# Larger token chunks, weight low parts on VectorE and 64x32 array tiles for the scores, in attention followed by two gated layers

## The chip, the cores and the metric

One core of a Trainium2 chip. The metric is the device time of one execution in microseconds (us), the median of several runs. A core has TensorE (PE, products; its weight loads are listed as PEld), VectorE (DVE), ScalarE (ACT), GpSimd (POOL) and SyncE (SP, which here only issues the DMAs). Each engine takes its instructions in the order in which the program lists them; semaphores make one engine wait for another.

## The reference

```python
# B, H, SL, SG, D = 4, 8, 512, 32, 64
s_g = scale * q_g @ k_all.T                    # 32 global queries see all 544 keys
out_g = softmax(s_g) @ v_all
s_ll = where(|i - j| <= 32, scale * q_l @ k_l.T, -1e9)   # local queries see a band
s_l = concat([scale * q_l @ k_g.T, s_ll])      # and the 32 global keys
out_l = softmax(s_l) @ concat([v_g, v_l])
x = attention output as (2304 tokens, 512)     # here 17 tiles of 128 tokens are processed
h = x @ w_in;  x = (h * clip(h + 3, 0, 6) / 6) @ w_out     # layer 1, d_ff 2048
h = x @ w_in2; x = where(h > 0, h, exp(min(h, 0)) - 1) @ w_out2   # layer 2
```

The inputs are float32, but the weights arrive as float64. The batch of 4 has 16 tiles of 128 local queries and one tile with all 128 global queries: 17 tiles, 2176 tokens.

## The kernel before

**Products.** A float32 operand is split into a high part (float32r) and a low part, the rest; a product is three matmuls: high by high, high by low, low by high (`mm3`, L385 to L389). All products of the two layers stand on L389 and differ by tile: `h` is the first product of a layer (`up`), `acc` the second (`down`).

**Chunks.** The 17 tiles are processed in chunks, `CHUNKS = [3, 3, 3, 2, 3, 3]`. For each chunk a layer makes one pass over d_ff in 16 steps (f) of 128. A step has `up` (12 matmuls with the chunk's tokens as columns: 384 or 256), an activation, and `down` (in layer 1 four blocks of 3 matmuls with the tokens as columns; in layer 2 one block of 3 matmuls with 512 columns per tile), which runs `LAG = 2` steps after its `up`. Between the parts of a step are three gaps: after `up`, after the first half of `down`, and after its second half. All work that isn't a product is written into these gaps by hand (the loop at L532): stages of attention for the next chunk's tiles (`during`, L487), ticks of splitting weights, loads.

**Activation of a step.** ACT makes g from h (L403 in layer 1; L406, L407 in layer 2), DVE finishes it (L404, L408), ACT writes the high part gh (L409), and the low part gl = g - gh (L411) is made by POOL in chunk 0 of layer 1 and by DVE elsewhere. `down` waits for gl.

**Weights.** One slot holds 128 of d_ff: 512 columns' worth of w_in and of w_out, 1 MB as float64 words. `Split` makes float32 from these words and then a high and a low part: `first` (ACT, L100), `second` (DVE, L104), `third` (DVE, L108 and L111), `fourth` (ACT copies the high part, L121; POOL subtracts the low part in two halves, L123). `tick` (L129) runs two such stages of neighbouring slots. Slots 0 and 1 of layer 1 are split by halves before the first product, the others during chunk 0, one slot per step and two steps ahead of their use. Layer 2's slots are split from step 4 of layer 1's last chunk on, at one and a half ticks a step.

**Attention of a local tile** (class `Local`, L159) has six stages. `scores` twice (L198; half of the heads each): 8 matmuls of a 128-row operand, q laid out block-diagonally for the two heads of a pair, into 64 output rows (column tiles of 64), 128 keys as columns; each float32 matmul is two records in the trace. Then a masked reduction (DVE, L218), the exponential with its sum (ACT, L222), 1/sum (DVE, L225, L226) and the scaling of P (POOL, L229; DVE for the tiles before the first product). `transposed` twice (four transposes L74, an ACT copy L239). `values` (L242): 32 matmuls in column tiles of 32, 64 value columns each, an ACT copy of x (L256). `turned`: four transposes, the ACT cast x1h (L263), the DVE subtraction x1l (L264). The tiles of chunk 0 do this before the first product, in the order of the string `PRO` (L38); the other tiles in the gaps of the chunk before theirs, at places (0, 2, 4, 7, 9, 11) with a step of 6 from tile to tile (L481), so that neighbouring tiles interleave. A global job (class `Global`) has three stages; `GLOBALS` says how many run in which chunk.

**Buffers and queues.** PSUM has 8 banks: 4 `acc`, 2 `h`, 2 `att`. The stages during the chunks use `att`. Tiles before the first product lie in the buffers of the weight slots (`w`). When a chunk ends, its accumulators are copied to `ev` (four buffers; ACT L437 and DVE L439 by turns) and stored; layer 1's results go to DRAM and come back as layer 2's input. SyncE issues all DMAs in program order.

Of the kernel before, what the change touches and what calls it, by code (L numbers as in the profile page):

```python
# [10 lines left out]
F32 = mybir.dt.float32  # L11
# [31 lines left out]
# A float64's upper word, read as float32, has the upper 8 of its 11 exponent bits as its exponent;  # L43
# times this it has them less 896 = 1023 - 127.
# [9 lines left out]
def tile_kernel(ctx, tc, qkW, vW, qkG, vN, vG, masks, w1, w2, out):  # L54
# [10 lines left out]
    msk = pool.tile([P, 3, 2, P], F32, name="msk")  # L65
# [63 lines left out]
    def tick(m, times=1):  # L129
        """The next two stages of splitting the weights of layer m, of slots that follow each other."""  # L130
# [28 lines left out]
    class Local:  # L159
        """Attention of 128 local queries, all heads, cut into stages."""  # L160

        def __init__(self, n):
# [3 lines left out]
            self.p = {}  # L166

        def load_qk(self):
            tag, bufs = ("w", NF) if self.early else ("qk", 1)
            qk = pool.tile([P, 2, 2, 2 * P + WIN], F32, name=f"qk{self.n}", tag=tag, bufs=bufs)  # L170
            src = qkW[self.b, self.t]
            if self.n == 0:
                nc.sync.dma_start(qk[:, 0], src[:, 0])
                nc.sync.dma_start(msk, masks)
                nc.sync.dma_start(qk[:, 1], src[:, 1])
            else:
                nc.sync.dma_start(qk, src)
# [12 lines left out]

        def buffer(self, name, tag, part):
            if not self.early:
                return pool.tile([P, 2, 2, P], F32, name=name, tag=tag, bufs=2)
            if not self.p:
                self.room = pool.tile([P, 4, 2, 2, P], F32, name=f"room{self.n}", tag="w", bufs=NF)
            return self.room[:, 2 * (tag == "pt") + part]

        def scores(self, part, tag):  # L198
            """Two pairs of heads: rows are (block of a half, head of the pair, query)."""
            sp = bank([P, 2, 2, P], f"S{self.n}_{part}", tag)  # L200
            for j in range(2):
                for i in range(4):
                    r = i % 2 * 64
                    nc.tensor.matmul(  # L204
                        sp[r : r + 64, j, i // 2, :],
                        self.q[:, part, j, i, :],
                        self.k[:, part, j, 32 * i : 32 * i + P],
                        start=True,
                        stop=True,
                    )  # L210
            p = self.buffer(f"P{self.n}_{part}", "p", part)
            mn = pool.tile([P, 4], F32, name=f"mn{self.n}_{part}", tag="mn", bufs=2)
            sums = pool.tile([P, 4], F32, name=f"sums{self.n}_{part}", tag="sums", bufs=2)
            mi = 0 if self.t == 0 else (2 if self.t == TPB - 1 else 1)
            for j in range(2):
                for hf in range(2):
                    c = slice(2 * j + hf, 2 * j + hf + 1)
# [10 lines left out]
            pf = p.rearrange("p j f k -> p (j f) k")  # L228
            eng.tensor_tensor(pf, pf, sums.unsqueeze(2).to_broadcast([P, 4, P]), op=ALU.mult)  # L229
            self.p[part] = p  # L230

        def transposed(self, part, tag):
            p = self.p[part]
            tp = bank([P, 2, 2, P], f"T{self.n}_{part}", tag)
            for j in range(2):
                for hf in range(2):
                    transpose(tp[:, j, hf, :], p[:, j, hf, :])
            pt = self.buffer(f"PT{self.n}_{part}", "pt", part)
            nc.scalar.copy(pt, tp)  # L239
            self.p[part] = pt  # L240
# [420 lines left out]
```

## Time and profile before

| | |
|---|---|
| median of 3 runs | 925.02 us (923.87 to 925.42) |
| span of the profiled execution | 923.7 us |
| difference, for what lies around the span | 1.3 us |
| start of the first product of layer 1 | 32.55 us |
| windows of layer 1, chunks 0 to 5 | 104.22, 88.28, 86.92, 65.09, 82.98, 67.58 us |
| first chunk of layer 2 | 527.62 to 601.25, 73.63 us |
| busy: PE, DVE, ACT, POOL | 883.6, 411.6, 424.1, 183.6 us |

The profile gives no time of the profiled execution other than its span, so the span stands for it. A window of a chunk runs from its first `up` matmul to that of the next chunk; it holds 16 ups of the chunk, 14 of its downs and the last 2 downs of the chunk before. Matmuls overlap in the array, so the price of one is the distance between starts and not its duration.

### The profile page before, as it was taken

The numbers are of one execution on the slowest core, as the hardware profiler recorded it, in microseconds if no ns is written. First come the engines' busy times: TensorE is split into PE (matmuls) and PEld (weight loads), VectorE is DVE, ScalarE is ACT, GpSimd is POOL, SyncE is SP. The second block draws the span as 40 slices with busy tenths as digits, with TensorE's granted clock in tenths as the row PEclk, the third lists the DMA queues.
The fourth block names the chain that finished last, engine by engine and source line by source line (L and its number), as shares of the span: only waits on it lengthen the run. The fifth ranks groups of instructions, "written<-read, shape, count | busy, mean of one in ns | idle before, by whom it ended". The sixth has DMA issues, their size and how long they took to land.

```text
span 923.7 us, 15740 instructions
## 1 busy us (share of the span) xinstructions
PE 883.6 (96%) x6432; PEld 811.8 (88%) x6432; DVE 411.6 (45%) x911; ACT 424.1 (46%) x944; POOL 183.6 (20%) x124
## 2 busy tenths in 40 slices
PE   6588799999999999999999989999999999999998
PEld 4477799989989999999999979999999999989997
DVE  4988864332432343432339978432222232322222
ACT  5666645433532354443335566533443444434433
POOL 0489781100100010000006644300100101001000
PEclk9799899999999999999999989999999999999999
DMA  9766313331423235232056630020010020100100
GB/s 371 319 270 225 135 47 109 131 122 45 134 80 130 65 124 164 89 101 67 1 179 238 259 140 18 18 69 0 1 57 1 1 69 1 57 1 1 35 1 34
DMA packets 21816, 90.27 MB, mean 98 GB/s; under 512 B 2544, under 2 KB 5872, under 8 KB 17264
## 3 DMA queue, kind: packets, MB, share of 16 engines
q1 hardware_dynamic: 21744, 89.27, 27.1%
q8 instruction: 50, 0.82, 0.4%
q14 instruction: 22, 0.18, 0.1%
HBM read 80.35 MB, written 8.91 MB: 97 GB/s over the span
## 4 chain that ended last, share of the span: by engine, by line
PE 80%; DVE 10%; ACT 5%; issue 4%; POOL 1%; DMA 0%; ACTq 0%; DVEq 0%
PE acc L389 36%; PE h L389 36%; DVE f L108 4%; DVE f L111 3%; PE S L204 3%; DVE f L104 1%; PE O L248 1%; PE T L74 1%; DVE g L404 1%; ACT P L222 1%; PE SG L316 1%; ACT room L222 1%; PE OG L346 1%; ACT w L121 1%; ACT gh L409 0%
## 5 line engine op out<-in xcount | busy, mean ns | idle before, releaser
L389 PE MATMUL acc<-gh,w 128*128 128x384 f32 (+1 forms) x768 | 213.9, 337 | 0.0
L389 PE MATMUL h<-x1h,w 128*128 128x384 f32 (+1 forms) x768 | 209.6, 338 | 4.0 <-POOL w L123 2.8
L389 PE MATMUL h<-x2h,w 128*128 128x384 f32 (+1 forms) x768 | 203.5, 330 | 0.0
L389 PE MATMUL acc<-w,gh 128*128 128x512 f32 x544 | 171.9, 397 | 3.3 <-ACT ev L437 3.3
L409 ACT CAST gh<-g 128x384 fp32r<-128x384 f32 (+1 forms) x192 | 95.1, 495 | 153.9 <-DVE g L404 90.9
L389 PEld LDWEIGHTS h<-x1h,w 128*128 128x128 f32 x768 | 140.0, 191 | 10.1 <-POOL w L123 3.5
L389 PEld LDWEIGHTS acc<-gh,w 128*128 128x128 f32 x768 | 139.3, 189 | 5.0 <-issue 3.8
L389 PEld LDWEIGHTS h<-x2h,w 128*128 128x128 f32 x768 | 138.7, 189 | 4.1
L408 DVE SCALAR_TENSOR_TENSOR g<-g,h 128x384 f32<-128x384 f32 (+1 forms) x96 | 51.1, 532 | 199.2 <-ACT g L407 199.2
L389 PE MATMUL h<-x1l,w 128*128 128x384 f32 (+1 forms) x384 | 127.6, 332 | 4.5 <-DVE x1l L264 4.5
L411 DVE TENSOR_TENSOR gl<-g,gh 128x384 fp32r<-128x384 f32 (+1 forms) x176 | 95.6, 543 | 77.1 <-ACT gh L409 77.0
L389 PE MATMUL acc<-gl,w 128*128 128x384 f32 (+1 forms) x384 | 126.9, 330 | 2.6 <-POOL gl L411 2.6
L123 POOL TENSOR_TENSOR w<-f,w 128x512 fp32r<-128x512 f32 x64 | 110.9, 1753 | 89.7 <-ACT w L121 89.7
L389 PE MATMUL h<-x2l,w 128*128 128x384 f32 (+1 forms) x384 | 126.7, 330 | 0.0
L404 DVE SCALAR_TENSOR_TENSOR g<-g,h 128x384 f32<-128x384 f32 (+1 forms) x96 | 50.9, 530 | 154.7 <-ACT g L403 154.6
L389 PEld LDWEIGHTS acc<-w,gh 128*128 128x128 f32 x544 | 101.1, 190 | 19.4 <-ACT ev L437 3.6
L406 ACT ACTIVATE g<-h 128x384 f32<-128x384 f32 (+1 forms) x96 | 45.5, 474 | 145.2 <-PE h L389 145.2
L403 ACT ACTIVATE g<-h,half 128x384 f32<-128x384 f32 (+1 forms) x96 | 53.9, 562 | 119.2 <-PE h L389 116.5
L389 PE MATMUL acc<-w,gl 128*128 128x512 f32 x272 | 108.1, 398 | 0.0
L464 POOL TENSOR_TENSOR x2l<-x2raw,x2h 128x768 fp32r<-128x768 f32 (+1 forms) x12 | 21.9, 1823 | 325.2 <-ACT x2h L463 325.2
L229 POOL TENSOR_TENSOR P<-P,sums 128x512 f32<-128x512 f32 x26 | 31.2, 1198 | 246.0 <-DVE sums L226 221.3
L389 PEld LDWEIGHTS h<-x1l,w 128*128 128x128 f32 x384 | 73.3, 191 | 4.9 <-DVE x1l L264 4.9
(72 smaller groups left out, 918.8 us busy)
## 6 DMA issues: line engine op xcount, KB each, us to landing
raw<-in_w SPq DMA_DIRECT2D x32, 1024.0 KB, 6.7
qk<-in_qkW SPq DMA_DIRECT2D x15, 960.0 KB, 4.8
v<-in_vW SPq DMA_DIRECT2D x26, 512.0 KB, 4.9
qkG<-in_qkG SPq DMA_DIRECT2D x8, 608.0 KB, 3.8
vN<-in_vN SPq DMA_DIRECT2D x8, 512.0 KB, 4.7
out<-ev SPq DMA_DIRECT2D x16, 256.0 KB, 2.1
x2d<-ev SPq DMA_DIRECT2D x20, 192.0 KB, 2.1
x2raw<-x2d SPq DMA_DIRECT2D x10, 384.0 KB, 3.7
```

Of the source, the lines that this page charges most:

```text
L108: nc.vector.scalar_tensor_tensor(w, self.high[:, s], -0x80000000, w, op0=ALU.bitwise_and, op1=ALU.bitwise_or)
L111: nc.vector.scalar_tensor_tensor(w, self.low[:, s], 29, w, op0=ALU.logical_shift_right, op1=ALU.bitwise_or)
L123: nc.gpsimd.tensor_sub(lo[:, i], self.wf[:, i], hi[:, i].bitcast(F32))
L204: nc.tensor.matmul(sp[r : r + 64, j, i // 2, :], self.q[:, part, j, i, :], self.k[:, part, j, 32 * i : 32 * i + P], start=True, stop=True,)
L229: eng.tensor_tensor(pf, pf, sums.unsqueeze(2).to_broadcast([P, 4, P]), op=ALU.mult)
L389: nc.tensor.matmul(o, a, b, start=first and i == 0, stop=last and i == len(pairs) - 1)
L403: nc.scalar.activation(g, hp, AF.Relu, scale=1.0 / 6.0, bias=half)
L404: nc.vector.scalar_tensor_tensor(g, g, 1.0, hp, op0=ALU.min, op1=ALU.mult)
L406: nc.scalar.activation(g, hp, AF.Relu, scale=-1.0)
L408: nc.vector.scalar_tensor_tensor(g, g, -1.0, hp, op0=ALU.add, op1=ALU.max)
L409: nc.scalar.copy(gh, g)
L411: late.append(lambda: eng.tensor_sub(gl, g, gh.bitcast(F32)))
```

## The change

The chunks become 4, 3, 3, 3, 4 tiles, and layer 2 takes them in the order 1, 0, 2, 4, 3. Four tiles instead of three are attended to before the first product, in a new order. In layer 1 DVE instead of POOL subtracts the weights' low parts. A local tile has four stages: all scores in one, from a q without zeros, in eight array tiles of 64 rows by 32 columns whose row halves write to two banks; all eight transposes in one; values with a 65th column of ones, whose result is the sum of the exponentials, so that the scaling comes after the values; and the turning. Stages during the chunks stand at places (0, 4, 6, 8) with a step of 9, those of global jobs at (0, 3, 5) instead of (0, 4, 8).

```diff
-CHUNKS = [3, 3, 3, 2, 3, 3]
+CHUNKS = [4, 3, 3, 3, 4]
+ORDER2 = [1, 0, 2, 4, 3]
-PRO = "q0 q1 v0 q2 v1 00 01 10 02 11 03 20 v2 12 04 13 21 05 W4 14 a100 a200 a101 W a201 a300 15 22 a110 a111 a301 a400 a210 a211 a310 23 w1 24 a311 a401 w1 q3 25 a410 a411 w1 w1 w1 | W | | | | | w1 w1 | w1 | w1 v3 |"
+PRO = "q0 q1 v0 q2 v1 00 v2 10 01 q3 W4 20 11 02 a100 a200 v3 a101 a201 30 03 21 a300 12 a110 a111 a301 31 a400 22 13 a210 a211 a310 23 32 a311 a401 33 a410 a411 w1 w1 q4 w1 w1 | W | | | | | w1 w1 | w1 | w1 v4 |"
-GLOBALS = [0, 2, 3, 1, 2]
+GLOBALS = [0, 3, 3, 2]
...
-                nc.gpsimd.tensor_sub(lo[:, i], self.wf[:, i], hi[:, i].bitcast(F32))
+                (nc.gpsimd if self.m else nc.vector).tensor_sub(lo[:, i], self.wf[:, i], hi[:, i].bitcast(F32))
...
-        xh = pool.tile([P, KD, n], F32R, name=f"x{which}h{c}", tag="xh", bufs=2)
+        side = "ab"[c % 2 if which == 1 else 1 - ORDER2.index(c) % 2]
+        xh = pool.tile([P, KD, n], F32R, name=f"x{which}h{c}", tag=f"xh{side}", bufs=1)
...
-            qk = pool.tile([P, 2, 2, 2 * P + WIN], F32, name=f"qk{self.n}", tag=tag, bufs=bufs)
+            qk = pool.tile([P, NP, P + WIN], F32, name=f"qk{self.n}", tag=tag, bufs=bufs)
...
-            self.v = [pool.tile([P, TPB, 4, D], F32, name=f"v{self.n}_{i}", tag="v", bufs=2) for i in range(2)]
+            tag, bufs = ("w", NF) if self.early else ("vw", 1)
+            self.v = pool.tile([P, TPB, H, D + 1], F32, name=f"v{self.n}", tag=tag, bufs=bufs)
...
+            sp = [bank([P, NP, P], f"S{self.n}_{r}", tag) for r in range(2)]
+            for j in range(NP):
                 for i in range(4):
+                    for r in range(2):
+                        rs, cs = slice(64 * r, 64 * r + 64), slice(32 * i, 32 * i + 32)
+                        nc.tensor.matmul(
+                            sp[r][cs, j, :], self.q[rs, j, cs], self.k[rs, j, 32 * i : 32 * i + P],
+                            start=True, stop=True,
+                        )
+            for j in range(NP):
+                for r in range(2):
                     nc.vector.tensor_tensor_reduce(
+                        out=self.p[:, r, j, :], in0=sp[r][:, j, :], in1=msk[:, mi, :], scale=-SCALE, scalar=BIG,
+                        op0=ALU.add, op1=ALU.min, accum_out=mn[:, r, j : j + 1],
                     )
                     nc.scalar.activation(
-                        p[:, j, hf, :], p[:, j, hf, :], AF.Exp, scale=-1.0, bias=mn[:, c], accum_out=sums[:, c]
+                        self.p[:, r, j, :], self.p[:, r, j, :], AF.Exp, scale=-1.0, bias=mn[:, r, j : j + 1]
                     )
-            nc.vector.tensor_scalar_add(sums, sums, 1e-9)
-            nc.vector.reciprocal(sums, sums)
-            eng = nc.vector if self.early else nc.gpsimd
-            eng.tensor_tensor(pf, pf, sums.unsqueeze(2).to_broadcast([P, 4, P]), op=ALU.mult)
+        def transposed(self, tag):
+            for r in range(2):
+                tp = bank([P, NP, P], f"T{self.n}_{r}", tag)
+                for j in range(NP):
+                    transpose(tp[:, j, :], self.p[:, r, j, :])
+                nc.scalar.copy(self.pt[:, r], tp)
+        def values(self, tag):
+            op = [bank([P, NP, D + 1], f"O{self.n}_{r}", tag) for r in range(2)]
+            for r in range(2):
+                for j in range(NP):
+                    for i in range(4):
+                        cs = slice(32 * i, 32 * i + 32)
+                        nc.tensor.matmul(
+                            op[r][cs, j, :], self.pt[:, r, j, cs], self.v[:, i, 2 * j + r, :], start=True, stop=True
+                        )
+                nc.vector.tensor_scalar_add(sums[:, r], op[r][:, :, D], 1e-9)
+            nc.vector.reciprocal(sums, sums)
-            nc.scalar.copy(self.x, op)
+            for r in range(2):
+                nc.vector.tensor_tensor(
+                    self.x[:, :, r, :], op[r][:, :, :D], sums[:, r].unsqueeze(2).to_broadcast([P, NP, D]), op=ALU.mult
+                )
...
-        ev = pool.tile([P, n if m == 0 else DM], F32, name=f"ev{m}_{c}_{i}", tag="ev", bufs=4)
+        ev = pool.tile([P, n if m == 0 else DM], F32, name=f"ev{m}_{c}_{i}", tag="ev", bufs=3)
...
-            place, step = ((0, 2, 4, 7, 9, 11), 6) if isinstance(job, Local) else ((0, 4, 8), 6)
+            place, step = ((0, 4, 6, 8), 9) if isinstance(job, Local) else ((0, 3, 5), 6)
...
-        first = [locs[n].stages(tags=("acc", "acc", "att", "att", "h", "h")) for n in range(CHUNKS[0])]
+        first = [locs[n].stages(tags=("acc", "att", "h", "acc")) for n in range(CHUNKS[0])]
...
-        order = [list(range(NC)), [*range(NC - 2), NC - 1, NC - 2]]
+        order = [list(range(NC)), ORDER2]
```

The tiles p and pt of a stage go from two buffers to one each; the host's layout of q, k, v and the masks follows the new shapes.

## Rows read from the trace of the kernel before

**Rows 1.** The page's busy times; the chain of waits, 30 to 140 us, by line.

```profile
PE 883.6 (96%) x6432; PEld 811.8 (88%) x6432; DVE 411.6 (45%) x911; ACT 424.1 (46%) x944; POOL 183.6 (20%) x124
...
by line: DVE f L108 20.0%; DVE f L111 14.8%; issue 13.1%; DVE f L104 9.3%; ACT P L222 8.0%; PE acc L389 5.9%; PE h L389 5.8%; DVE g L404 5.1%; POOL w L123 4.1%; ACT gh L409 2.4%; POOL gl L411 2.2%; ACT w L121 2.2%; DVE sums L225 2.0%; DVE x
```

**Rows 2.** Windows: length, busy of PE, PEld, DVE, ACT, POOL (count), clock, DMA, GB/s.

```profile
32.55:136.77 104.22, 86.34 (x684) 78.65 (x685) 86.43 (x125) 59.78 (x121) 84.18 (x53) 0.92 0.49 183
136.77:225.05 88.28, 88.28 (x815) 81.56 (x815) 30.49 (x115) 37.36 (x102) 7.53 (x7) 1.00 0.32 106
225.05:311.97 86.92, 86.16 (x761) 79.38 (x761) 29.80 (x104) 33.71 (x86) 4.30 (x4) 1.00 0.29 98
...
377.06:460.04 82.98, 82.98 (x717) 77.36 (x715) 30.20 (x103) 34.00 (x91) 4.30 (x4) 1.00 0.20 65
460.04:527.62 67.58, 67.58 (x386) 67.58 (x386) 48.98 (x56) 33.89 (x50) 27.40 (x15) 1.00 0.61 217
527.62:601.25 73.63, 70.31 (x343) 63.92 (x343) 52.94 (x61) 43.12 (x71) 33.29 (x22) 0.95 0.20 68
```

**Rows 3.** Timeline of PE in layer 2 (start us, length us, instruction).

```profile
733.77 0.62 PE L389 MATMUL acc<-w,gh 128*128 128x512 f32 x2
...
735.87 0.28 PE L389 MATMUL h<-x2h,w 128*128 128x256 f32 x1
...
737.30 0.63 PE L389 MATMUL acc<-w,gh 128*128 128x512 f32 x2
```

**Rows 4.** Timeline of PE in chunk 1 of layer 1: stages of attention between products.

```profile
142.04 0.34 PE L389 MATMUL acc<-gh,w 128*128 128x384 f32 x1
142.31 1.09 PE L204 MATMUL S<-qk 128*64 128x128 f32 x16
...
143.61 0.34 PE L389 MATMUL h<-x1l,w 128*128 128x384 f32 x1
...
147.66 0.60 PE L74 MATMUL T<-ident,P 128*128 128x128 f32 x4
...
148.27 0.33 PE L389 MATMUL h<-x1l,w 128*128 128x384 f32 x1
...
161.61 1.10 PE L248 MATMUL O<-v,PT 128*32 128x64 f32 x64
...
162.92 0.34 PE L389 MATMUL acc<-gl,w 128*128 128x384 f32 x1
```

**Rows 5.** Timeline of DVE, ACT and POOL around the first products.

```profile
28.21 0.68 DVE L264 TENSOR_TENSOR x1l<-XT,x1h 128x512 fp32r<-128x512 f32 x1
...
28.81 0.68 DVE L108 SCALAR_TENSOR_TENSOR f<-raw,f 128x512 int32<-128x512 int32 x1
...
37.05 0.68 DVE L264 TENSOR_TENSOR x1l<-XT,x1h 128x512 fp32r<-128x512 f32 x1
...
40.52 0.69 DVE L104 TENSOR_SCALAR f<-f 128x1024 int32<-128x1024 int32 x1
...
40.63 1.05 ACT L121 CAST w<-f 128x1024 fp32r<-128x1024 f32 x1 [3.48 <-DVE f L111]
...
41.24 1.23 DVE L108 SCALAR_TENSOR_TENSOR f<-raw,f 128x1024 int32<-128x1024 int32 x1
...
41.76 4.08 POOL L123 TENSOR_TENSOR w<-f,w 128x512 fp32r<-128x512 f32 x2 [3.50 <-ACT w L121]
...
42.50 2.19 DVE L111 SCALAR_TENSOR_TENSOR f<-raw,f 128x1024 int32<-128x1024 int32 x1
...
44.61 0.54 DVE L404 SCALAR_TENSOR_TENSOR g<-g,h 128x384 f32<-128x384 f32 x1
```

**Rows 6.** Timeline of PE at the start of layer 2; in brackets its wait.

```profile
541.66 1.22 PE L389 MATMUL acc<-w,gh 128*128 128x512 f32 x2 [3.32 <-ACT ev L437]
```

**Rows 7.** Weight loads before 24 us: their first issues, and issue to landing.

```profile
4.75 7.47 SPq L83 DMA_DIRECT2D raw<-in_w  x5
...
DMA to landing us min/median/max: 18.1/20.7/21.0
```

More of the change, by code (lines that the diff above doesn't have):

```diff
@@ L64, in tile_kernel @@
     ident = pool.tile([P, P], F32, name="ident")
-    msk = pool.tile([P, 3, 2, P], F32, name="msk")
+    msk = pool.tile([P, 3, P], F32, name="msk")
     half = pool.tile([P, 1], F32, name="half")
@@ L148, in x_tiles @@
         n = CHUNKS[c] * P
-        xh = pool.tile([P, KD, n], F32R, name=f"x{which}h{c}", tag="xh", bufs=2)
-        xl = pool.tile([P, KD, n], F32R, name=f"x{which}l{c}", tag="xl", bufs=2)
+        side = "ab"[c % 2 if which == 1 else 1 - ORDER2.index(c) % 2]
+        xh = pool.tile([P, KD, n], F32R, name=f"x{which}h{c}", tag=f"xh{side}", bufs=1)
+        xl = pool.tile([P, KD, n], F32R, name=f"x{which}l{c}", tag=f"xl{side}", bufs=1)
         return xh, xl
@@ L183, in load_v, with buffers @@
+            self.v = pool.tile([P, TPB, H, D + 1], F32, name=f"v{self.n}", tag=tag, bufs=bufs)
+            nc.sync.dma_start(self.v, vW[self.b, self.t])
+        def buffers(self):
             if self.early:
-                self.v = pool.tile([P, 2, TPB, 4, D], F32, name=f"v{self.n}", tag="w", bufs=NF)
-                nc.sync.dma_start(self.v, src)
-                return
-            self.v = [pool.tile([P, TPB, 4, D], F32, name=f"v{self.n}_{i}", tag="v", bufs=2) for i in range(2)]
-            for i in range(2):
-                nc.sync.dma_start(self.v[i], src[:, i])
@@ L191, in buffer @@
[L191 to L201, printed above, removed]
-                for i in range(4):
[L203 to L217, printed above, removed]
@@ new lines, in buffers, with scores @@
+                room = pool.tile([P, 2, 2, NP, P], F32, name=f"room{self.n}", tag="w", bufs=NF)
+                return room[:, 0], room[:, 1]
+            p = pool.tile([P, 2, NP, P], F32, name=f"P{self.n}", tag="p", bufs=1)
+            pt = pool.tile([P, 2, NP, P], F32, name=f"PT{self.n}", tag="pt", bufs=1)
+            return p, pt
+        def scores(self, tag):
+            self.p, self.pt = self.buffers()
+            sp = [bank([P, NP, P], f"S{self.n}_{r}", tag) for r in range(2)]
+            mn = pool.tile([P, 2, NP], F32, name=f"mn{self.n}", tag="mn", bufs=2)
+            mi = 0 if self.t == 0 else (2 if self.t == TPB - 1 else 1)
+            for j in range(NP):
+                for i in range(4):
+                    for r in range(2):
[6 more added lines that the diff above has]
+                for r in range(2):
@@ L224, in scores @@
                     )
-            nc.vector.tensor_scalar_add(sums, sums, 1e-9)
-            nc.vector.reciprocal(sums, sums)
-            eng = nc.vector if self.early else nc.gpsimd
-            pf = p.rearrange("p j f k -> p (j f) k")
-            eng.tensor_tensor(pf, pf, sums.unsqueeze(2).to_broadcast([P, 4, P]), op=ALU.mult)
[L230 to L240, printed above, removed]
@@ L242, in values @@
-        def values(self, tag):
-            op = bank([P, H, D], f"O{self.n}", tag)
-            for h in range(H):
-                pr, r = h // 2, 32 * (h % 2)
-                for i in range(4):
-                    c = i % 2 * 64 + r
-                    nc.tensor.matmul(
-                        op[32 * i : 32 * i + 32, h, :],
-                        self.p[pr // 2][:, pr % 2, i // 2, c : c + 32],
-                        (self.v[:, h // 4] if self.early else self.v[h // 4])[:, i, h % 4, :],
-                        start=True,
-                        stop=True,
-                    )
-            self.x = pool.tile([P, H, D], F32, name=f"x{self.n}", tag="x", bufs=1)
-            nc.scalar.copy(self.x, op)
+        def transposed(self, tag):
[4 more added lines that the diff above has]
+                nc.scalar.copy(self.pt[:, r], tp)
@@ L264, in turned, with stages, third @@
             nc.vector.tensor_sub(xl[:, :, c0 : c0 + P], xp, xh[:, :, c0 : c0 + P].bitcast(F32))
-        def stages(self, tags=("att",) * 6, nxt=None):
+        def stages(self, tags=("att",) * 4, nxt=None):
             def first():
-                self.scores(0, tags[0])
-            def second():
-                self.scores(1, tags[1])
+                self.scores(tags[0])
                 if nxt is not None:
                     nxt.load_qk()
-            def fifth():
-                self.values(tags[4])
+            def third():
+                self.values(tags[2])
                 if nxt is not None:
                     nxt.load_v()
-            return [
-                first, second,
-                lambda: self.transposed(0, tags[2]),
-                lambda: self.transposed(1, tags[3]),
-                fifth,
-                lambda: self.turned(tags[5]),
-            ]
+            return [first, lambda: self.transposed(tags[1]), third, lambda: self.turned(tags[3])]
     class Global:
@@ L576, in _masks @@
 def _masks():
-    m = np.full((2, 2, 32, 3, 2, 4, 32), -1.0e9 / SCALE, np.float32)
+    m = np.full((4, 32, 3, 4, 32), -1.0e9 / SCALE, np.float32)
     order = [0, 1, 2, "g", 3, 4, 5]
@@ L584, in _masks @@
                 lb = order[i + w]
[L585 removed]
+                blk = m[i, :, kind, w, :]
                 if lb == "g":
```

46 lines of the change are left out of this document (19 added, 27 removed).

## The prediction

> **What bounds the kernel now.** The page's busy times and the windows by chunk come first [rows 1, 2]. TensorE (PE) is busy 883.6 of 923.7 us, but the windows show two kinds of stretch. In chunks 1, 2 and 4 of layer 1 PE is busy for (nearly) the whole window and the clock is 1.00: what lengthens these chunks is PE's own attention work. Chunk 0 is different: VectorE (DVE) is busy 86.43 and GpSimd (POOL) 84.18 of 104.22 us, and the chain of waits from 30 to 140 us has 44% in the splitting operations L108, L111 and L104 on DVE [rows 1].
>
> Three prices follow. A product with 384 columns costs 67.58/(16 x 24) = 0.176 us, from the last chunk of layer 1, which has no attention [rows 2]. Nine of 512 columns take 735.87 - 733.77 = 2.10, so 0.2333 each; twelve of 256 take 1.43, so 0.119 [rows 3]. A stage of attention costs PE what it puts between products: scores (S) 143.61 - 142.04 less two products = 1.22; four transposes (T) 148.27 - 147.66 less one = 0.434; values (O) take 162.92 - 161.61 = 1.31 from their start on where scores take 1.30, so 1.23 [rows 4]. A local tile (S, S, T, T, O, XT) thus costs 2 x 1.22 + 3 x 0.434 + 1.23 = 4.97. Check: chunk 1 is 88.28 - 67.58 = 20.7 over its products, three tiles make 14.9, and the two global jobs are left with 2.9 each.
>
> The time before, by parts: the first product can run when the low part of tile 2 lands, 37.05 + 0.68 = 37.7 [rows 5]; chunk 0 then has 99.0 us for 30 groups of products (63.4) and three tiles (14.9), so it stalls 20.7. Layer 2's first chunk takes 73.63 against 16 x (12 x 0.176 + 9 x 0.2333) = 67.4: it loses 6.3, beginning with a wait of 3.32 for a copy on ScalarE (ACT), after which the clock is at 0.95 for the window [rows 2, 6]. The span is 923.7, the median 925.0; I add the difference, 1.3, at the end.
>
> **The change part by part.**
>
> *Chunks.* Layer 1: before 384 x (5 x 0.176 + 0.119) = 383.7, after 384 x (3 x 0.176 + 2 x 0.2333) = 382.0. The up half of layer 2: 191.9 to 191.0; its down half has 512 columns either way. Together **-2.6**.
>
> *Attention on PE.* One more tile goes ahead of the first product, so 12 local tiles are on PE's path instead of 13. O keeps its 64 records (65 columns for 64), the eight transposes cost 0.87, XT 0.434. S is the open price: the two stages (32 records) become one of 64 records, eight small tiles of the array. Rows 4 have the nearest cases: with two column tiles 16 records of 128 columns take 1.09, with four column tiles 64 records of 64 columns take 1.10. So tiles in other columns do run side by side; no row shows two row halves doing so. If all eight run together, 64 records are eight waves as now: 1.22. If the halves take turns, there are eight waves more, at 0.434/4 = 0.109 each: 2.09. If nothing overlaps, 56 more: 7.3. I take 1.22, as column tiles overlap fully and the two halves write to two banks. A tile then costs 1.22 + 0.87 + 1.25 + 0.43 = 3.77: 13 x 4.97 = 64.6 becomes 12 x 3.77 = 45.2, **-19.4**. The globals are unchanged.
>
> *One serial chain in two banks.* S, T, O each take both "att" banks and XT one, and place and step (0, 4, 6, 8; 9) no longer interleave tiles. In chunks 1 to 3 the next S stands one gap after XT. XT needs 0.60 on PE, ACT's x1h about 0.6 (half as wide as L121, 1.05), DVE's x1l 0.68 before its bank is free [rows 4, 5]: 1.9 us, while PE has 0.43 + 6 x 0.176 = 1.49 to do. About 0.5 for nine tiles: **+5** (2 to 8). DVE takes over the scaling: two additions, a reciprocal and two products of 256 columns, none above the 0.54 of g [rows 5], so at most 2.7, I take 1.4; in chunks 1 to 3 DVE is a third busy and hides it. POOL's scaling, ACT's copy of x and the exponentials' sums go from engines that have room. The tile's v comes in one load instead of two behind one buffer; O stands nine gaps of 1.4 us after the load's release, so SyncE's queue hides it.
>
> *Prologue.* Four tiles instead of three. The loads ahead of the first weights are a little smaller (6.28 for 6.49 MB), so these land near 4.75 + 18.1 - 0.5 = 22.3 instead of 22.9 [rows 7]. But in the new order the first split stands ahead of the scores of tile 3 on ACT and DVE, which therefore wait for that landing. Behind it DVE has four half slots of L104 (0.35 each) and of L108 with L111 (1.3), two subtractions and four x1l (0.6), tile 3's score reductions (1.7, below) and three values stages (1.4): 16.1 us, and an estimated 1.6 of waits for ACT (half an L100 at the head, x1h): 17.7 after the landing the first product has all it needs, at 40.0. Against 37.7: **+2.3** (0 to 5). POOL is idle there, so nothing slows DVE.
>
> *Chunk 0.* The low parts move from POOL (two in 4.08 where DVE is also busy) to DVE. Per slot DVE then has L104 0.72, L108 1.26, L111 1.26, two subtractions at 0.60 (x1l's starts, 28.21 to 28.81): 4.4. These subtractions stand right behind L111 in DVE's queue and read ACT's high copy of its result (1.05, L121): a new wait of about 1.1 at the head of DVE's queue, with the next slot's L104 and the next g behind it. With g (0.6): 6.1. POOL keeps g's low part, 512 wide, at most half of 4.08 = 2.0 us a step, and slows DVE while it runs (L111 took 2.19 under POOL, L108 1.23 without: 0.44 of the overlap is lost), at most 0.9; I take 0.6, as a part falls into DVE's waits: 6.7. Attention: chunks 1 and 2 leave DVE 13.1 and 12.4 us beside g and gl (1.1 a step), so a local tile holds it some 3 us (x1l 0.68, the sums' four small operations about 0.6, the eight score reductions the other 1.7), 3.7 after the change: 0.7 a step, a third of it inside the new wait. Sum 7.2 a step. PE has 24 x 0.2333 + 3 x 3.77/16 = 6.3. For the 13 steps that still split, DVE's chain leads by 0.9: a stall of 12 instead of 20.7, **-9** (stall 3 to 20).
>
> *Layer 2's start.* Same work, but the chunk before it has steps of 5.6 instead of 4.2 for ACT and DVE to catch up. I take a loss of 3 for 6.3: **-3.3** (0 to 7 lost). The ev buffers go from four to three: the fourth copy now waits for the first store, but its bank is wanted only after the next up and half a down, 12 x 0.176 + 6 x 0.176 = 3.2 us on, which covers it; if not, it lies within the 7.
>
> Sum: -2.6 - 19.4 + 5 + 2.3 - 9 - 3.3 = -27.0: 923.7 - 27.0 + 1.3 = **898**.
>
> **Rivals.**
> - *The row halves take turns.* S costs 2.09: 12 x 0.87 = +10.4, so 908. Against it: column tiles overlap in rows 4. The Trainium skill ("TensorE: Matmul & The Clock Gate", section "Wait — 56ns, not 53.3ns?") speaks against the change in a like way: matmuls never start less than about 25 ns apart. An estimate by that page is 64 x 0.025 = 1.6 for the records of S instead of 0.87, which would make the time about 907. The trace doesn't agree: the 64 records of O take 1.10 in all, 17 ns each. Chance 0.17.
> - *DVE keeps up in chunk 0.* If its waits fall into PE's time and POOL hardly disturbs it, the stall is 2 or 3: 888. For it: 6.7 a step without attention is near PE's 6.3. Chance 0.2.
> - *Slower: the eight array tiles run one after another.* Each S is then 64 waves of 0.109: 6.1 more a tile, 12 x 6.1 = 73, so 971. It decides from S = 1.22 + 27/12 = 3.5 us on. For it: no row has row tiles of 64; against it, all column tiles. Chance 0.05.
>
> **How the numbers follow.** The forecast, 898, has 0.58. Its own bounds give 883 (stall 3, chain 2, nothing lost at layer 2) and 910; the first two rivals lie inside or near, and both unfavourable together give 914. The range is 882 to 914; outside it are the slower rival and combinations of ends. A measurement of this kernel can tell about 0.2%. Faster 0.94: the forecast and the first two rivals, less a little for small mishaps that would add up; same 0.01; slower 0.05.
>
> **What would show it.** Right: the S row with 64 records in about 1.1 us; chunks 1 to 3 at about 90, 89 and 87 us with PE nearly full; layer 1's last chunk at about 88 and unbroken; in chunk 0 DVE waits for L121 ahead of the subtractions, POOL is mostly idle, and steps are near 7; the first product is complete near 40. Wrong: S near 2 us or more, an idle PE ahead of S or O in chunks 1 to 3 beyond 1 us a tile, chunk 0 above 115 us, or a first product after 45.

## The result and the profile after

The changed kernel takes 895.65 us (895.24 to 897.35, four runs) where the kernel before takes 924.44 on the same chip: a ratio of 0.9693 [0.9679, 0.9706]. The forecast was 898.0 in a range of 882 to 914. The profiled execution took 895.24 us and has a span of 893.2.

In the new file the products of both layers stand on L368, scores S on L206, all transposes on L76, values O on L235; a slot's split is L102 (first, ACT), L106 (second), L110 and L113 (third), L123 (high copy, ACT), L125 (low part).

The page's busy times of the kernel after, then its chain of waits from 30 to 140 us by line, as in [rows 1]:

```profile
PE 858.7 (96%) x6368; PEld 740.9 (83%) x6368; DVE 407.3 (46%) x888; ACT 385.8 (43%) x715; POOL 94.6 (11%) x64
...
by line: DVE f L113 26.4%; DVE w L125 17.1%; DVE f L110 15.6%; ACT w L123 10.5%; DVE f L106 8.0%; DVE g L383 6.6%; ACT P L216 4.1%; issue 3.3%; DVE x L242 3.1%; DVE x1l L252 1.8%; DVE P L212 1.5%; DVE sums L239 1.0%; DVE sums L238 0.7%; ACT
```

In this stretch VectorE's splitting (L113, L110, L106, L125) is 67% of the chain, and another 10.5% is ScalarE's high copy L123, for which VectorE waits. In [rows 1] the splitting was 44%, and GpSimd's low parts (L123 there) another 4.1%.

Windows of the kernel after, with the columns of [rows 2]: layer 1's five chunks, then layer 2's first (chunk 1):

```profile
40.31:152.50 112.19, 102.40 (x780) 78.62 (x781) 93.69 (x156) 61.35 (x95) 22.59 (x16) 0.96 0.40 152
152.50:242.50 90.00, 89.63 (x964) 81.26 (x963) 34.53 (x127) 34.63 (x79) 0.96 (x1) 1.00 0.34 112
242.50:331.13 88.63, 88.21 (x964) 80.98 (x964) 34.76 (x128) 34.41 (x79) 0.00 (x0) 1.00 0.33 111
331.13:417.78 86.65, 86.25 (x919) 80.24 (x919) 35.24 (x127) 34.83 (x83) 0.00 (x0) 1.00 0.25 84
417.78:504.98 87.20, 87.20 (x385) 71.94 (x385) 53.46 (x60) 39.96 (x53) 27.34 (x16) 1.00 0.50 171
504.98:574.50 69.52, 68.77 (x343) 61.74 (x342) 49.85 (x57) 41.64 (x68) 30.83 (x20) 1.00 0.22 76
```

In chunks 1 to 4 TensorE is busy for all but 0.5 us of each. Chunk 0 is not so full: four tiles want 15 x 24 x 0.230 = 82.8 us of products and 3 x 3.86 = 11.6 of attention (both prices below), and from its first complete product at 41.3 it has 111.2. It stalls some 17 us. Of these about 2 go with a low clock at its head: up to the first scores the granted clock is 0.52 (the lower of its two levels, 1.2 GHz, but for the last moment; TensorE had been idle for 3.3 of the 4.2 us ahead), and eleven products of 512 columns take 4.86 us, for 2.5 in later steps. The kernel before begins in the same way (0.55 from 37.70 to 43.00).

```profile
40.31:46.19 5.88, 5.65 (x12) 3.76 (x12) 5.22 (x7) 3.67 (x5) 0.00 (x0) 0.52 0.01 1
```

Layer 2's first chunk is nearly whole; its clock no longer falls [rows 2, 6].

Timeline of TensorE in chunk 1 of the kernel after: the stages of one local tile (its scores with the products around them), then the first scores of the next one, which are cut in two:

```profile
154.44 0.34 PE L368 MATMUL h<-x1h,w 128*128 128x384 f32 x1
154.71 1.16 PE L206 MATMUL S<-qk 64*32 64x128 f32 x64
155.79 0.50 PE L368 MATMUL acc<-gh,w 128*128 128x512 f32 x1
156.13 0.39 PE L368 MATMUL acc<-gl,w 128*128 128x512 f32 x1
...
160.77 1.04 PE L76 MATMUL T<-ident,P 128*128 128x128 f32 x8
...
164.49 1.12 PE L235 MATMUL O<-v,PT 128*32 128x65 f32 x64
...
168.82 0.63 PE L76 MATMUL XT<-ident,x 128*128 128x128 f32 x4
...
170.44 0.40 PE L206 MATMUL S<-qk 64*32 64x128 f32 x2
171.00 1.14 PE L206 MATMUL S<-qk 64*32 64x128 f32 x62 [0.17 <-DVE x1l L252]
```

The 64 records of S take 1.16 us where 16 records took 1.09 in [rows 4]: the eight array tiles run together. (Record by record, the first 32 start in groups of eight, 6 or 7 ns apart within a group and 0.11 to 0.13 us from group to group.) The last two lines are the new chain: two records go, the others wait for the bank of `XT`, which VectorE's x1l still reads.

Timeline of VectorE, then ScalarE, then GpSimd, in one step of chunk 0 of the kernel after:

```profile
52.82 0.69 DVE L383 SCALAR_TENSOR_TENSOR g<-g,h 128x512 f32<-128x512 f32 x1 [1.93 <-ACT g L382]
53.43 1.22 DVE L110 SCALAR_TENSOR_TENSOR f<-raw,f 128x1024 int32<-128x1024 int32 x1
54.68 2.21 DVE L113 SCALAR_TENSOR_TENSOR f<-raw,f 128x1024 int32<-128x1024 int32 x1
58.00 1.29 DVE L125 TENSOR_TENSOR w<-f,w 128x512 fp32r<-128x512 f32 x2 [1.11 <-ACT w L123]
59.21 0.69 DVE L106 TENSOR_SCALAR f<-f 128x1024 int32<-128x1024 int32 x1
59.81 0.68 DVE L383 SCALAR_TENSOR_TENSOR g<-g,h 128x512 f32<-128x512 f32 x1
...
56.92 1.04 ACT L123 CAST w<-f 128x1024 fp32r<-128x1024 f32 x1 [1.70 <-DVE f L113]
...
54.24 1.56 POOL L390 TENSOR_TENSOR gl<-g,gh 128x512 fp32r<-128x512 f32 x1 [3.01 <-ACT gh L388]
```

A step without attention is 59.81 - 52.82 = 6.99 us of VectorE, by starts: 0.61 + 1.25 + 2.21 + a wait of 1.11 + 1.21 + 0.60. TensorE wants 24 x 0.230 + 11.6/16 = 6.2. L110 and L113 are of one shape; L113 takes 1 us longer, and it is the one that runs while GpSimd makes gl (54.24 to 55.80).

### The profile page after: what moved, and what is told of

Read it like the earlier page. It is cut to its first block, busy times and chain, and to the rows that moved or that the text cites. A ratio compares the mean times of both kernels' runs of the same rounds, so it can differ in the third digit from the quotient of the medians.

```text
span 893.2 us, 15162 instructions
## 1 busy us (share of the span) xinstructions
PE 858.7 (96%) x6368; PEld 740.9 (83%) x6368; DVE 407.3 (46%) x888; ACT 385.8 (43%) x715; POOL 94.6 (11%) x64
## 4 chain that ended last, share of the span: by engine, by line
PE 75%; DVE 15%; ACT 5%; DMA 2%; issue 2%; SPq 1%; ACTq 0%; DVEq 0%
PE h L368 35%; PE acc L368 34%; DVE f L113 4%; DVE f L110 4%; DVE w L125 2%; ACT w L123 2%; DMA raw<-in_w 2%; DVE g L383 1%; DVE f L106 1%; PE S L206 1%; PE SG L295 1%; PE O L235 1%; PE T L76 1%; PE OG L325 1%; DVE x1l L252 1%
## 5 line engine op out<-in xcount | busy, mean ns | idle before, releaser
L368 PE MATMUL h<-x1h,w 128*128 128x384 f32 (+1 forms) x640 | 197.8, 370 | 4.5 <-ACT w L123 3.8
L368 PE MATMUL acc<-gh,w 128*128 128x384 f32 (+1 forms) x640 | 198.7, 366 | 0.0
L368 PE MATMUL h<-x2h,w 128*128 128x384 f32 (+1 forms) x640 | 191.3, 360 | 0.0
L368 PE MATMUL acc<-w,gh 128*128 128x512 f32 x544 | 169.4, 392 | 0.3 <-DVE ev L418 0.3
L368 PEld LDWEIGHTS h<-x1h,w 128*128 128x128 f32 x640 | 119.7, 190 | 24.9 <-ACT w L123 5.3
L368 PEld LDWEIGHTS acc<-gh,w 128*128 128x128 f32 x640 | 118.8, 188 | 12.4 <-issue 1.0
L368 PEld LDWEIGHTS h<-x2h,w 128*128 128x128 f32 x640 | 118.3, 188 | 12.8
L368 PEld LDWEIGHTS acc<-w,gh 128*128 128x128 f32 x544 | 101.6, 188 | 19.8 <-DVE ev L418 0.7
L368 PE MATMUL h<-x1l,w 128*128 128x384 f32 (+1 forms) x320 | 116.4, 364 | 0.2 <-DVE x1l L252 0.2
L368 PE MATMUL acc<-gl,w 128*128 128x384 f32 (+1 forms) x320 | 115.0, 360 | 0.0
L368 PE MATMUL h<-x2l,w 128*128 128x384 f32 (+1 forms) x320 | 114.8, 359 | 0.0
L383 DVE SCALAR_TENSOR_TENSOR g<-g,h 128x384 f32<-128x384 f32 (+1 forms) x80 | 48.5, 606 | 134.1 <-ACT g L382 133.6
L368 PE MATMUL acc<-w,gl 128*128 128x512 f32 x272 | 106.9, 393 | 0.5 <-DVE gl L390 0.5
L368 PEld LDWEIGHTS h<-x2l,w 128*128 128x128 f32 x320 | 60.2, 188 | 7.5
L368 PEld LDWEIGHTS h<-x1l,w 128*128 128x128 f32 x320 | 61.0, 191 | 6.1 <-DVE x1l L252 0.7
L368 PEld LDWEIGHTS acc<-gl,w 128*128 128x128 f32 x320 | 60.4, 189 | 5.0
```

Source lines behind the costliest of these rows:

```text
L368: nc.tensor.matmul(o, a, b, start=first and i == 0, stop=last and i == len(pairs) - 1)
L383: nc.vector.scalar_tensor_tensor(g, g, 1.0, hp, op0=ALU.min, op1=ALU.mult)
```

## The experiments

Ratios are to the kernel before, run on the same chip (923.95 to 925.41 us).

**The moved subtraction.** One line: GpSimd subtracts layer 1's low parts again, the rest as after.

```diff
-(nc.gpsimd if self.m else nc.vector).tensor_sub(lo[:, i], ...)
+nc.gpsimd.tensor_sub(lo[:, i], ...)
```

> The changed kernel with the low parts of layer 1's weights back on POOL. Theory (DVE's queue sets chunk 0: two subtractions of 0.6 and a wait of 1.1 us per slot stand in it): chunk 0 falls from 112 us by some 8 to 10, as DVE loses 2.3 us a step and gets about 1.4 back as contention from a busier POOL; 885 to 889 us. Rival (POOL's subtractions were what held chunk 0 before, and moving them is a gain): POOL is busy over 80% of chunk 0 again, PE waits for L125 there, 897 to 903 us.

Measured: 886.87 us, 0.9607 [0.9584, 0.963], as the theory has it. The move costs 8 us by the ratios, 9 by the medians. Chunk 0 in a window, then the costliest lines of VectorE and of GpSimd in it, of this kernel:

```profile
40.08:144.38 104.30, 100.71 (x780) 79.60 (x781) 86.95 (x125) 61.41 (x95) 80.49 (x46) 0.95 0.43 163
...
L113 DVE SCALAR_TENSOR_TENSOR f<-raw,f 128x1024 int32<-128x1024 int32 x14 | 29.8, 2130 | 0.5
L110 DVE SCALAR_TENSOR_TENSOR f<-raw,f 128x1024 int32<-128x1024 int32 x14 | 21.0, 1499 | 0.0
L106 DVE TENSOR_SCALAR f<-f 128x1024 int32<-128x1024 int32 x14 | 16.4, 1171 | 1.4 <-ACT f L102 1.4
...
L125 POOL TENSOR_TENSOR w<-f,w 128x512 fp32r<-128x512 f32 x30 | 49.3, 1662 | 20.9 <-ACT w L123 20.7
```

The same lines of VectorE in chunk 0 of the kernel after:

```profile
L113 DVE SCALAR_TENSOR_TENSOR f<-raw,f 128x1024 int32<-128x1024 int32 x14 | 28.0, 2003 | 0.5
L125 DVE TENSOR_TENSOR w<-f,w 128x512 fp32r<-128x512 f32 x31 | 20.1, 687 | 13.2 <-ACT w L123 13.2
L110 DVE SCALAR_TENSOR_TENSOR f<-raw,f 128x1024 int32<-128x1024 int32 x14 | 18.1, 1294 | 0.0
...
L106 DVE TENSOR_SCALAR f<-f 128x1024 int32<-128x1024 int32 x14 | 9.6, 686 | 0.0
```

With GpSimd at work, L106, L110 and L113 lose 29.8 + 21.0 + 16.4 - 28.0 - 18.1 - 9.6 = 11.5 us. With the low parts on VectorE it spends 20.1 on them and stands 13.2 before them. So the contention that the move takes away is real, but it is less than the 33 us that VectorE pays for it.

**The old chunks.** The new attention and VectorE's subtraction, with the chunks, `GLOBALS`, layer 2's order and the buffers' sides of before, and a `PRO` for three tiles of the new attention:

```diff
-CHUNKS = [4, 3, 3, 3, 4]
+CHUNKS = [3, 3, 3, 2, 3, 3]
-ORDER2 = [1, 0, 2, 4, 3]
+ORDER2 = [0, 1, 2, 3, 5, 4]
...
```

> The changed kernel with the chunks of before (3, 3, 3, 2, 3, 3), three tiles ahead of the first product. Theory (chunk 0's steps are set by DVE's chain of about 7 us, whatever the width, so a fourth tile's products in chunk 0 come nearly free): chunk 0 takes 103 to 107 us for three tiles and PE idles over 25 us in it; 908 to 914 us. Rival (the chunks are worth only the narrower products and one tile of attention, 2.6 + 3.8 us, and the shorter prologue gives 2 to 3 back): 899 to 903 us.

Measured: 917.11, 0.9923 [0.9908, 0.9938], above both expectations.

**The attention alone.** The same with the low parts on GpSimd. What is left of the change is the attention and what came with it: three `ev` buffers, and the wider v, whose effect on the weight slots the last experiment measures (2 us).

> The chunks of before, the low parts on POOL as before, only the new attention. Theory: chunks 1 to 4 take the 313 us that they took with the old chunks and DVE's subtractions (323 before), and chunk 0 gains too, since DVE no longer waits for the exponentials and POOL no longer scales P: 8 to 14 us less than its 104 with the start 4 to 5 us earlier; 898 to 906 us. Rival (chunk 0 is set by POOL's subtractions and L110, L113 under them, which are unchanged): chunk 0 stays near 104 and only its start is earlier, 908 to 912 us.

Measured: 905.17, 0.9792 [0.9778, 0.9807], in the theory's range. The window of chunk 0 with the old chunks (three tiles), first with VectorE's subtraction, then with GpSimd's:

```profile
27.66:140.06 112.40, 86.39 (x780) 80.13 (x781) 84.54 (x163) 57.33 (x96) 15.24 (x16) 0.89 0.46 174
```

```profile
28.48:128.66 100.18, 84.27 (x780) 76.94 (x781) 88.31 (x132) 57.55 (x96) 81.01 (x47) 0.93 0.50 191
```

With VectorE's subtraction chunk 0 takes 112.40 us for three tiles and 112.19 for four, or 109.2 and 111.2 from the first complete product on: VectorE's and ScalarE's chain sets it, and the fourth tile's work on TensorE comes nearly free. By medians: the attention 924 to 905 (-19), larger chunks on top of it to 886.9 (-18), the moved subtraction to 895.65 (+9; +12 with the old chunks). Layer 2's loss at its start is there with the old chunks (its first chunk takes 73.30 and 73.35 us) and goes with the new ones. TensorE's line from 515 to 545 us of the kernel with old chunks and VectorE's subtraction:

```profile
L368 PE MATMUL acc<-w,gh 128*128 128x512 f32 x12 | 5.2, 525 | 3.7 <-ACT ev L416 3.7
```

It is the wait of [rows 6]; in the kernel after the longest wait in that chunk is 0.5.

**Row halves one after the other.** In the scores the loop over the two row halves goes outermost.

```diff
-for j in range(NP):
-    for i in range(4):
-        for r in range(2):
+for r in range(2):
+    for j in range(NP):
+        for i in range(4):
```

> The changed kernel with the loop over the two row halves outermost in the scores, so that records in a row use the same 64 rows and only four column tiles can overlap. Theory (row halves overlap when they alternate): S grows from 1.16 to about 2.0 us, eight waves of 0.109 more; nine tiles in chunks 1 to 3 pay 0.87 each, chunk 0's three are partly hidden by DVE: 903 to 907 us. Rival (the 64 records are held by a fixed distance between starts of about 17 ns, with or without row tiles): S stays at 1.16, 895 to 897 us.

Measured: 895.90, 0.9691 [0.9676, 0.9705]; no difference to the kernel after. Its scores of a chunk's first and second tile:

```profile
154.60 1.56 PE L206 MATMUL S<-qk 64*32 64x128 f32 x64
...
170.73 1.64 PE L206 MATMUL S<-qk 64*32 64x128 f32 x64
```

The time agrees with the rival, the reason doesn't. The order does matter: 1.56 instead of 1.16 where nothing waits, so the halves overlap only in part (the first records now start in groups of four, not eight). But for the second and third tile of a chunk the first half needs only the bank that is free, and its work covers the wait: S puts 1.70 us between products there, 1.76 after. So only a chunk's first tile pays; chunks 1 to 3 together take 266.1 us for 265.3, too little to tell in the time of the whole.

**Places.** S two gaps behind XT instead of one.

```diff
-place, step = ((0, 4, 6, 8), 9) if isinstance(job, Local) else ((0, 3, 5), 6)
+place, step = ((0, 3, 5, 7), 9) if isinstance(job, Local) else ((0, 3, 5), 6)
```

> The changed kernel with a local tile's stages at places (0, 3, 5, 7) instead of (0, 4, 6, 8), so that two gaps lie between XT and the next S. Theory (S waits for DVE's x1l of the tile before, 0.55 to 0.6 us, twice in each of chunks 1 to 3): those six waits go, S stays at 1.16: 3 to 4 us less, 891.5 to 893 us. Rival (the wait moves: T or O, one gap nearer to the stage ahead of them, or the global job's S, take it over): 895 to 896 us.

Measured: 899.72, 0.9734 [0.972, 0.9749], slower than after. Neither expectation holds. The window of chunk 0, then TensorE and ScalarE in chunk 1 of this kernel:

```profile
40.62:156.28 115.66, 106.62 (x780) 80.11 (x781) 93.25 (x156) 61.76 (x95) 22.34 (x16) 0.93 0.40 147
...
174.76 1.14 PE L206 MATMUL S<-qk 64*32 64x128 f32 x62 [0.20 <-DVE x1l L252]
...
172.99 0.52 ACT L388 CAST gh<-g 128x384 fp32r<-128x384 f32 x1 [0.62 <-DVE g L383]
173.41 0.58 ACT L251 CAST x1h<-XT 128x512 fp32r<-128x512 f32 x1
```

XT (from 171.52) now stands just after an `up`, and ScalarE makes g and gh of that step ahead of x1h. The bank is free as much later as S was moved, the wait stays, and a transpose waits for exponentials besides (0.22 us in chunk 2). That is the lesser part: chunks 1 to 3 take 0.9 us more in all. Chunk 0, of which neither expectation spoke, takes 3.5 more, at a clock of 0.93 for 0.96; which of its waits does it was not followed up.

**Both of these.** GpSimd's subtraction together with the new places.

> The low parts back on POOL and the places (0, 3, 5, 7) together. Theory (two separate stretches: chunk 0 and chunks 1 to 3): the gains add, 883 to 884 us. Rival (the places also matter in chunk 0, where the stages then meet DVE's backlog earlier): 885 to 888 us.

Measured: 891.07, 0.9638 [0.962, 0.9656]: 4 us above GpSimd's subtraction alone, and above both expectations. Chunk 0 takes 106.2 us for 104.3, which is the rival's reason; in the profiled execution the first product also stands 2.4 later, and why was not followed up.

**The wait for the high copy.** In an odd tick the next slot's L106 goes ahead of the low parts, so that VectorE has work while ScalarE copies.

```diff
-now = (((k - 3) // 2, Split.fourth), ((k - 1) // 2, Split.second))
+now = (((k - 1) // 2, Split.second), ((k - 3) // 2, Split.fourth))
```

> The changed kernel with the two stages of an odd tick swapped: the next slot's L106 (0.7 us) goes ahead of the subtractions L125 in DVE's queue and fills most of their 1.11 us wait for ACT. Theory (DVE's chain with that wait sets chunk 0): 0.6 to 0.7 us less in each of about 11 steps, 887 to 890 us. Rival (PE's own steps of 6.3 or POOL's gl set chunk 0): under 2 us, 893.5 to 896 us.

Measured: 889.20, 0.9623 [0.9609, 0.9637], in the theory's range; chunk 0 takes 106.13. The wait in its timeline:

```profile
62.69 0.68 DVE L106 TENSOR_SCALAR f<-f 128x1024 int32<-128x1024 int32 x1
63.88 1.29 DVE L125 TENSOR_TENSOR w<-f,w 128x512 fp32r<-128x512 f32 x2 [0.51 <-ACT w L123]
```

It falls from 1.11 to 0.51, by the 0.60 that L106 takes from its start to the next one (59.21 to 59.81 in the kernel after).

**The contention.** The low part gl of chunk 0 on VectorE, so that GpSimd is idle there.

```diff
-eng = nc.gpsimd if (m, c) == (0, 0) else nc.vector
+eng = nc.vector
```

> The changed kernel with g's low part in chunk 0 made by DVE instead of POOL, which then has nothing to do there. Theory (POOL's gl, 1.5 us a step, is what stretches L113 from 1.22 to 2.2): L113 falls to 1.22 to 1.25, DVE gains 1.0 a step and pays 0.6 to 0.7 for gl, and gl stands in DVE's queue ahead of the splitting: 2 to 5 us less, 890 to 893.5 us. Rival (L113 is slow by its own operands): L113 stays at 2.2, DVE's chain grows by 0.65 a step, 903 to 906 us.

Measured: 889.69, 0.9625 [0.9609, 0.9641], a little better than the theory's 890 to 893.5; chunk 0 takes 106.04. VectorE's rows from 60 to 140 us of this kernel:

```profile
L113 DVE SCALAR_TENSOR_TENSOR f<-raw,f 128x1024 int32<-128x1024 int32 x12 | 14.7, 1225 | 0.4
L110 DVE SCALAR_TENSOR_TENSOR f<-raw,f 128x1024 int32<-128x1024 int32 x12 | 14.6, 1219 | 0.0
```

L113 is back at L110's time. VectorE does 0.68 us more a step and loses 1 less.

**Both cures.**

> Both cures of chunk 0 with the low parts left on VectorE: second ahead of fourth in a tick, and g's low part of chunk 0 on VectorE. Theory (one chain on VectorE sets chunk 0; its wait for ScalarE's high copy and the slowing of L113 by GpSimd are separate terms of it): the two gains of some 6 us add, chunk 0 takes 98 to 102 us instead of 111, the time is 882 to 885, and L113 is at 1.2 us. Rival (one cover for both: once one of them is gone TensorE or ScalarE sets the step): 886 to 890, chunk 0 at 104 to 107, like either alone.

Measured: 885.75 (885.58 to 886.55), 0.9575 [0.9561, 0.959]: 10 us below the kernel after, the fastest of all here, though its interval meets that of GpSimd's subtraction alone. Chunk 0 takes 102.89, between the two expectations: of 6.4 and 6.0 us some 10 remain. Its window, and pieces of its chain of waits from 60 to 140 us:

```profile
40.22:143.11 102.89, 100.40 (x781) 79.27 (x781) 91.25 (x172) 61.63 (x95) 0.00 (x0) 0.95 0.44 165
```

```profile
105.39 1.15 DVE f L110
...
109.04 1.14 PE S L206 x62
110.18 2.98 PE acc L368 x12
113.15 2.73 PE h L368 x12
```

From 109 us on the chain is TensorE's alone; before that it is still VectorE's for the most part. With GpSimd's subtraction alone it goes over to TensorE at 110. So two ways to a shorter chain end at the same next bound.

**Other divisions between the two engines.** Low parts on GpSimd with gl on VectorE; then, with the order of the tick changed, the low part of the first half on VectorE and of the second on GpSimd.

> Layer 1's weights' low parts back on GpSimd, g's low part of chunk 0 on VectorE. Theory (in this form VectorE, slowed by GpSimd, still sets chunk 0): GpSimd loses 1.56 of its 5 us a step but VectorE takes on 0.6, so that the gain over the first of the two alone (886.87) is small: 884 to 888. Rival (GpSimd's own chain sets it: its subtraction of a slot is late for the product): 878 to 883, chunk 0 below 100 us.

> Second ahead of fourth, and the low part of the first half of a slot on VectorE, that of the second half on GpSimd. Theory (what GpSimd does at the same time costs VectorE about as much as it takes off it): VectorE saves 0.6 us a step and loses as much again in L106 to L113, so 887 to 891, no better than with the order alone (889.20). Rival (shared work is best): 881 to 885.

Measured: 890.43 (0.9626 [0.961, 0.9642]) and 890.13 (0.9621 [0.9606, 0.9636]). The second went as its theory has it. The first missed both expectations, being by the medians 3.6 us slower than with gl on GpSimd; its first product stands 1.4 us later and chunk 0 is 0.8 longer, and why was not followed up.

**The spacing of the slots.** The kernel before with a single edit: the early v is allocated as wide as in the kernel after. It shares its buffers with the weights.

```diff
-self.v = pool.tile([P, 2, TPB, 4, D], F32, name=f"v{self.n}", tag="w", bufs=NF)
+slot = pool.tile([P, 8 * TPB * (D + 1)], F32, name=f"v{self.n}", tag="w", bufs=NF)
+self.v = slot[:, : 8 * TPB * D].rearrange("p (a b c d) -> p a b c d", a=2, b=TPB, c=4)
```

> The kernel before, with one edit: the early tiles of v are allocated with 65 columns a head (the last 128 bytes are unused), so that the sixteen weight slots, which share that tag, stand 8320 bytes apart instead of 8192. Theory (that spacing is why attention-free steps of three tiles take 4.15 to 4.21 us in the kernel after, where all take 4.21 in the one before): the same steps here take 4.15 to 4.21 us, layer 2's second chunk 66.9 instead of 67.3, and the time is 919 to 923. Rival (the steps are shorter for another reason): all stay at 4.21, 924 to 926.

Measured: 922.22, 0.9976 [0.9967, 0.9985]; the gain is 2 us, as the theory has it. Layer 2's second chunk in this kernel, then in the kernel before:

```profile
601.37:668.36 66.99, 66.99 (x338) 60.68 (x336) 18.39 (x33) 26.94 (x53) 3.69 (x2) 1.00 0.07 24
```

```profile
601.25:668.56 67.31, 67.31 (x338) 60.92 (x336) 18.41 (x33) 26.91 (x53) 3.67 (x2) 1.00 0.07 24
```

Its steps take 4.16 to 4.21 us, by the slot, where all took 4.21; in the kernel after such steps take 4.15 to 4.21. The edit also moves whatever lies behind the slots, so the spacing and the place as such are not parted.

## Why the prediction was right, and where its terms were off

The span fell by 923.7 - 893.2 = 30.5 us; the prediction had 27.0. Term by term, with prices from the starts of the products, in both kernels:

| term | predicted | measured |
|---|---|---|
| chunks (products) | -2.6 | -10.1 |
| attention on PE | -19.4 | -18.6 |
| serial chain in two banks | +5 | +3.5 |
| prologue | +2.3 | +3.6 |
| chunk 0's stall | -9 | -3.8 |
| layer 2's start | -3.3 | -5.0 |
| sum | -27.0 | -30.4 |

The scores of the global jobs, which have no term, take 0.5 less. That the forecast came within 3 us is in part luck: the products gained 7.5 more than forecast and chunk 0's stall 5.2 less, and these two errors nearly cancel.

- **Chunks.** Mis-sized, by the prices: a step of four tiles without attention takes 5.52 us, 0.230 for each of 24 products of 512 columns and not the 0.2333 of [rows 3], and one of three tiles 4.18 to 4.19 for 4.21 to 4.23 before. The sum of such steps comes to -10.1. The last experiment shows where the second gain comes from, an effect of the change that the prediction didn't see. Why 512 columns are cheaper is open: the steps of four tiles also differ by the slot (5.44 to 5.59 us, and the longest is 0.233 a product), which speaks for the same effect, but in the last experiment the chunk of two tiles took 46.60 us, as before.
- **Attention on PE.** Right. A stage costs what it puts between the products, and the product behind it is slower too: the next one follows it by 0.28 us (behind S and O) or 0.26 (behind transposes), for 0.175 elsewhere. The line behind the first S of [rows 4] is this:

```profile
143.33 0.44 PE L389 MATMUL h<-x1h,w 128*128 128x384 f32 x1
```

The next one starts at 143.61. The prediction's 1.22 and 0.434 took in both parts. Over all undisturbed tiles the same sum gives 2 x 1.22 + 2 x 0.44 + 1.23 + 0.44 = 4.99 before (4.97 predicted), and 1.29 (S) + 0.88 (T) + 1.25 (O) + 0.44 (XT) = 3.86 after (3.77 predicted). S, the open price, is 0.07 dearer than 1.22. So 13 x 4.99 - 12 x 3.86 = 18.6.

- **The serial chain.** Right in place and price: in chunks 1 to 3 the second and third tiles' S wait 0.58 each, six of the nine predicted. The others stand at the head of a chunk, with no XT ahead of them.
- **Prologue.** The weights landed later than estimated (ScalarE's first L102 waits for them until 23.14, for 22.3), and the first product was complete at 41.3 instead of 40.0.
- **Chunk 0.** Right in mechanism, mis-sized in the stall. VectorE's chain takes 7.32 us a step (L113 starts at 54.68 and, eleven slots on, at 135.25), and 7.2 was predicted; the new wait is the predicted 1.1. Inside this sum two errors partly cancel. "At most 0.9; I take 0.6" for the contention failed: L113 loses 1.0 in most steps (2.21 for 1.22), as gl falls almost wholly under it. And the attention adds 0.33 a step for the 0.5 that was left of 0.7: L125 doesn't wait at all behind the scaling of x (71.97), and half as long behind x1l (78.95), while once, where eight exponentials stand ahead of L123 on ScalarE, it waits longer (88.47):

```profile
71.97 1.29 DVE L125 TENSOR_TENSOR w<-f,w 128x512 fp32r<-128x512 f32 x2
...
78.95 1.29 DVE L125 TENSOR_TENSOR w<-f,w 128x512 fp32r<-128x512 f32 x2 [0.51 <-ACT w L123]
...
88.47 1.29 DVE L125 TENSOR_TENSOR w<-f,w 128x512 fp32r<-128x512 f32 x2 [1.97 <-ACT w L123]
```

So over 13 steps the chain leads TensorE's 6.2 by 1.1 and not 0.9, which makes 14, and the low clock at the head, for which the estimate of 12 had no term, adds some 2: together 16 of the 17 that it stalls. Measured in the same way the kernel before stalls 20.6. What the prediction didn't say is that the move by itself costs: it was priced together with the larger chunk, and the first experiment parts them.

- **Layer 2's start.** Right in sign; the loss is 1.3 and not 3 (69.52 us, where the later window of the same make-up, from 661.47 to 729.73, takes 68.26). The experiments with old chunks show that it hangs on the new chunks and their order; the reason given, the longer steps of a chunk of four tiles ahead of it, agrees with that, but was not tested by itself.

The rivals. "The row halves take turns" would have shown 2.09 in the row of S; it shows 1.16, and even with the halves issued apart 1.56. "Eight array tiles one after another" is out by the same row. The Trainium skill's floor of about 25 ns between starts of matmuls ("TensorE: Matmul & The Clock Gate", section "Wait — 56ns, not 53.3ns?") doesn't hold across array tiles here: 64 records in 1.16 us are 18 ns each, and within a group of eight the starts are 6 or 7 ns apart. "DVE keeps up in chunk 0" (888) describes no part of this kernel, but the two cures, which bring it nearer, take the time to 885.75.

## What to carry to other kernels

Price a move between engines alone, before adding what a larger tile hides in the same stretch: here the two were forecast together as a gain of 9 us, and the move's cost of 8 to 12 us inside it went unseen. Where an engine takes over work, count the wait for its input at the head of its queue, and put other ready work in front of it. And price a stage with the product behind it: measured only up to that product's start, each stage here would have seemed 0.1 us cheaper, 0.6 a tile before and 0.4 after.

## What the runs showed of the hardware

- **Array tiles.** Eight fp32 tiles of 64 x 32 in two banks run together: 64 records of 128 columns in 1.16 us, where 16 records with two column tiles took 1.09 [rows 4]. Issued half by half they still overlap in part (1.56).
- **The product behind a stage.** It holds up the next one: 0.28 us from start to start behind scores or values, 0.26 behind transposes, for 0.175 between other products of 384 columns, in both kernels. No run here says why.
- **VectorE beside GpSimd.** An int32 `scalar_tensor_tensor` of 128 x 1024 with both operands in SBUF takes 1.22 us alone and 2.2 beside a GpSimd subtraction of 1.56; L106 goes from 0.69 to 1.17 on average when GpSimd subtracts the weights; L383, with one operand in PSUM, stays at 0.69. The step shown above is much like a lock: had L113 (from 54.68) stood until gl's end at 55.80 and then taken its 1.22, it would have ended at 57.02; it ended at 56.89. L110, already running when gl began, kept its 1.22, and gl took 1.56 there, where it takes 1.27 to 1.30 if no L110 runs at its start. And where gl (141.85 to 143.12) begins ahead of L110 (142.21), it is L110 that takes 2.00. The Trainium skill has this as a rule ("SBUF — State Buffer", section "SBUF: two separate sides"): a VectorE instruction with two operands in SBUF and a GpSimd instruction that reads SBUF take a shared pair of ports by turns, each for its whole length. By it the contention would have been put at up to the whole of gl, and not at a share of its overlap.
- **Where the stationary operands lie.** Weight slots 8320 instead of 8192 bytes apart make steps of three tiles 0 to 0.05 us shorter (of 4.21), 2 us in all. No run here says by what mechanism, or whether the spacing does it or the moved places.
